# Keeping attention's result in SBUF as fp16 pairs instead of storing it to DRAM and loading it back, in a fused attention and MLP kernel

## Chip, core, metric

One core of a Trainium2 chip. The engines are TensorE (PE), VectorE (DVE), ScalarE (ACT), GpSimd (POOL) and SyncE (SP), which issues nearly all DMAs. The metric is the device time of one execution, in microseconds; lower is better.

## What is computed

```python
# attention, per batch b (4) and head h (8): S=576 tokens, D=64
scores = (q @ k.T) / sqrt(D) + (cum[:, None] - cum[None, :])   # cum = cumsum(log f)
attn = softmax(where(causal, -1e9, scores)) @ v
x = attn as [2304 tokens, 512]
# first MLP: 512 -> 2048 -> 512
g = leaky_relu(x @ moe_w_in, 0.01) ;  y = g @ moe_w_out
# second MLP: 512 -> 1024 -> 512
h = y @ moe2_w_in ;  solu = h * softmax(h)
out = (layernorm(solu) * g_ln) @ moe2_w_out
```

All inputs and the output are float32. The kernel keeps float32-like accuracy with pairs: a value is held as a high half and the rest as a low half, and a product is three matmuls (high by high, high by low, low by high).

## The kernel before

The program does not issue its instructions in the order of its text. Each step is recorded as an operation with an engine (or several to choose from), a duration guess, a priority (a lower number goes first) and the buffers it reads and writes. `Plan.run` (a list scheduler) then walks through modelled time, gives each free engine the ready operation with the best priority whose buffers can be had, and emits it. The order on each engine's queue is fixed by that; on the chip every queue runs strictly in order. `PASSES`, `UN`, `ORDER`, `WIP`, `WOP`, `LD...`, `PP...`, `WEIGHT`, `LAT` and the like are priorities and guesses for this planner. Buffers are tags with a number of slots; when a tag is used up, its slots go over to other tags (`heirs`).

**Attention** runs in eight passes, `PASSES`. Pass A of a batch does query blocks 0 and 1 (tokens 0 to 255) of its four head pairs, pass B blocks 2, 3 and the 64-row block 4. Per head: scores on PE into `ps_s`; mask and row extreme on DVE (L750); exp with row sum on ACT (L700); the guard, which adds 1e-9 to the sum and scales it (L709, L710 on DVE, or L712 ACT, L714 DVE or POOL); reciprocal (L718); high part `hl` (L453, L458) and low part (L464); a DMA transpose `pt<-hl` issued by SP; PV on PE into `ps_v`; eviction into `xr`, float32, on ACT and DVE (L781, L784). `V` is split into pairs in `split_v` (low parts L464 on DVE, or L467 and L468 on POOL).

**The way of x.** `pair` ends with a store of `xr` to the DRAM tensor `xs_d`. The first MLP works on nine token blocks of 256: block b and 4+b are tokens 0 to 255 and 256 to 511 of batch b, block 8 the last 64 tokens of all four batches. `load_x` waits for the stores of all four head pairs of a batch, loads the block back into an `xw` buffer (once `sd`, so the trace says `sd<-xs_d`), and splits it into two fp16 pair tiles `x` (copy L453 or L460, then subtraction L468).

**The first MLP** runs in units `(block, g)`, g being one of two halves of the hidden layer: g=0 holds the first `GA` groups of 256 hidden columns, g=1 the rest of eight. `hidden` makes one group (24 matmuls of 256 columns from `x`, then two ACT and one DVE operation into a pair `g`); after the groups of a unit come its y matmuls, added up in `yo`. Weights come as 32 chunks of 512 KB through three staging buffers `wst`, are joined and reduced on ACT, POOL and DVE, and are split into pairs in `wz` or `qa`. A half's output weights (`split_wo`) are scaled together, so its y matmuls need all chunks of that half. Units of this MLP run on PE between attention's matmuls, as filling, and after attention without a break. **The second MLP** follows, per 128 tokens.

**Start.** `decay` computes the cumulated log of f and writes two rows of 8 KB into `qa`, rows 64 and 65, by two small DMAs (`qa<-sd`); the first scores need them.

Of the kernel before, what the change touches and what calls it, by code (L numbers as in the profile page):

```python
# [7 lines left out]
F32 = mybir.dt.float32  # L8
# [19 lines left out]
NVT = 9  # L28
NRAW = 3
NWST = 3  # L30
ORDER = (0, 1, 4, 2, 5, 3, 6, 8, 7)
EARLY = 1779.78
NE = 2
NQK = 3
WST = 1.0
PA = 83.64

PASSES = (("A", 0, 127.52, 0.5), ("A", 1, 186, 3), ("B", 0, 200, 5), ("A", 2, 222, 8), ("B", 1, 256, 20), ("A", 3, 338, 8), ("B", 2, 372, 20), ("B", 3, 454, 20))
PP = -9.25
PV = -9.04  # L40
SM = 6.0
AV = -2.77
EP = 1726.79
LD = 60.42
LDV = 18.49
LDW = 5.82
KSTEP = 0.56
EPD = 11.22
URGENT = -1000.0
BACKLOG = 9115.27  # L50
LOP = 310.01
WIP = (120.0, 190.0)
WOP = (121.0, 190.14)
WIST = -3.25
WOST = 1.0
WSP = (122.0, 189.01)
GA = 3
UN = ((0, 0), (0, 1), (1, 0), (1, 1))
NYO = 2
NX = 3  # L60
NGT = 4
US0 = 17.36
HST = 2.0
TB = 256
NB = NT // TB
# [5 lines left out]
LNS = 1024.0  # L71
TOP = 14
GS = 2.0 ** -24
YD = 14.21
OLAG = 32.29

# [24 lines left out]
    __slots__ = ("eng", "dur", "emit", "bufs", "prio", "npred", "succ", "seq", "taken", "dma", "weight", "heat", "lock")  # L101


WEIGHT = {"DVE": 4.54}
WEIGHT2 = {"DVE": 1.9}
HEAT = 0.25
TOPE = 253.69
QUEUES = ("SP",)
SHARE = 0.62
PORT = 150.0  # L110
LAT = {"PE": 220.0, "ACT": 150.0, "DVE": 150.0, "POOL": 57}
WINDOW = 4096 / 1.2
HI_ENGS = ("ACT", "DVE")
UNITS = {2: ((0, 1),), 3: ((3,), (2,))}
V_ENGS = ("ACT", "DVE", "POOL")
VL_ENGS = ("DVE", "POOL")
HD4 = 0
REC_ENGS = ("DVE", "POOL", "ACT")
LO_ENGS = ("DVE", "POOL")
# [232 lines left out]
def dve(n):  # L352
    return 1.042 * n + 70
# [26 lines left out]
def body(tc, kqa, kq, vt, f, wa, w2i, w2o, gln, out):  # L380
# [10 lines left out]
    def tiles(pool, name, n, shape, dt):  # L391
        return [pool.tile(shape, dt, name=f"{name}{i}") for i in range(n)]
# [16 lines left out]
    ex = base.tile([128, 128], F32, name="ex")  # L409
    P.tag("ex", [ex])  # L410
    P.tag("turn", [ex])
    junk = base.tile([128, 512], BF16, name="junk")
    P.tag("va", tiles(base, "va", 2, [128, 1], F32R))

    xs_d = tiles(dram, "xs_d", B, [128, KD, S], F32)
    yp_d = tiles(dram, "yp_d", NB, [128, KD, TB], F32)
    dr_d = dram.tile([2 * NP, 4, KQ], F32, name="dr_d")

# [23 lines left out]

    halves = lambda t, dt: [t[:, 512 * j:512 * j + 512].bitcast(dt) for j in range(2)]
    as_g = lambda t: t.bitcast(F16).rearrange("p (j n) -> p j n", j=2)
    heirs("sd", "xw", "xw")
    heirs("dec", *[lambda t: [("g", as_g(t[:, 512 * j:512 * j + 512])) for j in range(2)]] * 2)
    heirs("wst", lambda t: [("yo", t[:, 512 * j:512 * j + 512].bitcast(F32)) for j in range(2)],
          *[lambda t: [(nm, as_g(t[:, 512 * j:512 * j + 512])) for j, nm in enumerate(("g", "x"))]] * 2)
    heirs("qa", lambda t: [("wz", t[:, h, p]) for h in range(2) for p in range(KD)])

    def copy_on(eng, o, i, scale=None):
# [79 lines left out]
    def decay():  # L531
# [161 lines left out]
    def softmax(parts, prio):  # L693
# [127 lines left out]
    def pair(p, prio, blocks):  # L821
        n0 = len(P.ops)
        b, kd = divmod(p, KD)
        full = len(blocks) == 2
        (prep_full if full else prep_split)(p, prio)
        xr = P.buf("xr")
        k = 0
        for hd in range(2):
            pts = {}
            for unit in UNITS[len(blocks)]:  # L830
                pts.update(scores(p, unit, hd, prio + SM + KSTEP * k, full))
                k += 1
# [134 lines left out]
    def load_x(blk, prio):
        xb = []
        deps = [o for b, a, c, o in spills if any(b == x and a <= s < c for x, s, _ in tokens(blk))]
        for q in range(2):  # L970
            xw, x = P.buf("xw"), P.buf("x")
            at = 0
            wide = lambda xw=xw: xw.t[:, 0:512].rearrange("p (a n) -> p a n", a=2)
            for b, s, n in tokens(blk):
                load((xw, at), lambda wide=wide, o=at, n=n: wide()[:, :, o:o + n],
                     lambda q=q, b=b, s=s, n=n: xs_d[b][:, 2 * q:2 * q + 2, s:s + n], 128 * 2 * n * 4, prio - 4000, deps=deps)
                at += n
            src = lambda xw=xw: xw.t[:, 0:512]
            copy_f(lambda x=x: x.t[:, 0], src, 512, prio - 3000, w=[(x, 0)], r=[xw])
            sub_f(lambda x=x: x.t[:, 1], src, lambda x=x: x.t[:, 0], 512, prio - 3000, w=[(x, 1)], r=[xw, (x, 0)])  # L980
            xb.append(x)
        return xb

    YPD, YP = {}, []

    XB, YO, LEFT = {}, {}, {}

    def ffn(blk, g, prio):
        eprio = prio - EP
        first, last = blk not in XB, LEFT.setdefault(blk, 2) == 1  # L990
        LEFT[blk] -= 1
        if blk < B:
            P.op(DVE, 140, lambda: nc.vector.tensor_scalar(ev(YS + 4 * g + blk), ev(EB + blk), ev(EZ + g), WSC * 2.0 ** (40 - 3 * TOP), op0=ALU.mult, op1=ALU.mult),
                 prio - 3000, w=[(EX, ("y", g, blk))], r=[(EX, ("b", blk)), (EX, ("z", g))])
        if first:
            XB[blk], YO[blk], YPD[blk] = load_x(blk, prio), [P.buf("yo") for q in range(2)], []
# [217 lines left out]
```

## Time and profile before

| | us |
|---|---|
| runs of the kernel before: median (lowest to highest of 3) | 789.78 (787.78 to 791.29) |
| the profiled execution: its time | 793.71 |
| the profiled execution: its span, first to last event | 791.9 |
| PE busy with matmuls in that span | 719.5 |
| DVE, ACT, POOL busy | 513.5, 467.3, 285.4 |

Read it so: the span is the time from the first to the last recorded event of one execution; its time includes 1.8 us around it. An engine's idle time is span less busy time. A matmul's end is modelled, so busy stretches of PE say that it was fed, not that it ran at its peak.

### The profile page before, as it was taken

What the parts mean: (1) busy time and instruction counts of PE and PEld (TensorE: products, weight loads), DVE (VectorE), ACT (ScalarE), POOL (GpSimd) and SP (SyncE); (2) the same over time, 40 slices, a digit from 0 to 9 for tenths busy, and PEclk for the clock granted to TensorE, in tenths of its full rate; (3) what the DMA queues carried; (4) which work ended last, traced back from release to release, by engine and by line L of the source; (5) the groups of instructions that cost most, each with busy time, mean ns of one, the idle gap of its engine ahead of it and who ended that gap; (6) DMA issues with size and microseconds to landing.
All of it is one profiled execution on the core that took longest, in us unless ns stands there. A gap on an engine that the chain in (4) does not pass through costs nothing.

```text
span 791.9 us, 15449 instructions
## 1 busy us (share of the span) xinstructions
PE 719.5 (91%) x5647; PEld 576.6 (73%) x5647; DVE 513.5 (65%) x1256; ACT 467.3 (59%) x1060; POOL 285.4 (36%) x341
## 2 busy tenths in 40 slices
PE   2453898999799999999999999999999999999997
PEld 1342787787688877888888888888887766666653
DVE  6888988977888777887883552115134675556651
ACT  2879989876889679988882563224221333233321
POOL 3839696723553076653513220001001233222020
PEclk9999999999999999999999999999999999999999
DMA  8798779568778778777866550000003334453224
GB/s 267 203 240 274 203 189 242 108 117 162 167 172 144 137 153 174 153 132 162 168 129 150 176 201 27 9 20 2 27 1 94 94 94 106 107 107 90 59 65 106
DMA packets 175277, 103.61 MB, mean 131 GB/s; under 512 B 147313, under 2 KB 155713, under 8 KB 175201
## 3 DMA queue, kind: packets, MB, share of 16 engines
q1 hardware_dynamic: 175200, 102.62, 55.8%
q8 instruction: 44, 0.72, 0.4%
q14 instruction: 33, 0.26, 0.1%
HBM read 52.67 MB, written 14.78 MB: 85 GB/s over the span
## 4 chain that ended last, share of the span: by engine, by line
PE 47%; DMA 2%; DVE 1%; ACT 0%; issue 0%; SPq 0%; ACTq 0%
PE ps_f L499 31%; PE ph L499 12%; PE ps_g L499 3%; DMA tr<-hl 1%; DMA pt<-hl 1%; PE ps_v L499 0%; PE ps_s L499 0%; DVE hl L464 0%; ACT ot L1098 0%; SPq L490 0%; DVE st L709 0%; ACT hl L453 0%; DVE ps_s L750 0%; DVE xr L784 0%; DVE st L718 0%
## 5 line engine op out<-in xcount | busy, mean ns | idle before, releaser
L499 PEld LDWEIGHTS <-wz 128*128 128x128 f16 x2808 | 273.6, 99 | 39.5 <-issue 6.8
L499 PE MATMUL ps_f<-x,wz 128*128 128x256 f16 x864 | 108.9, 278 | 0.0
L499 PE MATMUL ph<-w,y 128*128 128x512 f32 x432 | 103.7, 396 | 0.0
L464 DVE SCALAR_TENSOR_TENSOR hl<-ps_s,st,hl 128x512 f16<-128x512 f32 (+4 forms) x160 | 83.4, 538 | 17.3 <-ACT hl L453 15.9
L499 PEld LDWEIGHTS ph<-w,y 128*128 128x128 f32 x432 | 81.0, 188 | 18.1
L499 PE MATMUL ps_f<-wst,wz 128*128 128x256 f16 x696 | 90.0, 273 | 0.0
L700 ACT ACTIVATE ps_s<-ps_s,st 128x512 f32<-128x512 f32 (+4 forms) x160 | 78.4, 490 | 19.2 <-DVE st L750 11.4
L499 PE MATMUL ps_v<-pt,VT 128*128 128x128 f16 (+1 forms) x928 | 60.9, 218 | 28.7 <-DVE xr L784 14.5
L468 POOL TENSOR_TENSOR kq<-raw,kq 64x576 fp32r<-64x576 f32 (+1 forms) x60 | 74.4, 1246 | 25.7 <-ACT kq L453 22.9
L499 PE MATMUL ps_f<-g,wz 128*128 128x256 f16 x636 | 81.3, 273 | 1.3 <-DVE g L953 1.3
L499 PEld LDWEIGHTS <-VT 128*128 128x128 f16 x928 | 53.3, 101 | 38.0 <-issue 20.8
L499 PEld LDWEIGHTS <-tr 128*128 128x128 f16 x432 | 41.0, 98 | 53.0 <-issue 3.9
L453 ACT ACTIVATE hl<-ps_s,st 128x512 f16<-128x512 f32 (+3 forms) x128 | 67.0, 550 | 21.1 <-DMA pt<-hl 10.2
L499 PE MATMUL ps_f<-dec,wz 128*128 128x256 f16 x612 | 77.1, 273 | 0.0
L499 PEld LDWEIGHTS <-qa 128*128 128x128 f16 x648 | 61.9, 98 | 9.6 <-issue 2.5
L750 DVE CUSTOM_DVE_ANT_0 ps_s<-ps_s,mask 128x128 f32<-128x128 f32 (+3 forms) x128 | 62.4, 498 | 9.5 <-PE ps_s L499 7.3
L499 PE MATMUL ps_s<-kq 128*128 128x512 f32 (+5 forms) x256 | 64.3, 376 | 4.4 <-DVE hl L464 2.9
L453 ACT ACTIVATE hl<-raw 128x1024 f16<-128x1024 f32 x17 | 18.0, 1057 | 62.1 <-DMA tr<-hl 32.8
L499 PEld LDWEIGHTS ps_s<-kq 128*128 128x128 f32 (+1 forms) x256 | 41.5, 194 | 12.2 <-DVE hl L464 3.7
L1072 POOL TENSOR_SCALAR s<-s 128x1 f32<-128x1 f32 x18 | 4.4, 245 | 126.2 <-DVE s L1067 125.9
L1055 ACT ACTIVATE raw<-ph,s 128x1024 f32<-128x1024 f32 x18 | 20.0, 1113 | 39.6 <-DVE s L1053 39.6
L952 ACT ACTIVATE ps_f<-ps_f 128x512 f32<-128x512 f32 x72 | 42.5, 590 | 0.4
(176 smaller groups left out, 1193.9 us busy)
## 6 DMA issues: line engine op xcount, KB each, us to landing
wst<-wa SPq DMA_DIRECT2D x32, 512.0 KB
raw<-kq SPq DMA_DIRECT2D x16, 480.0 KB
VT<-vt SPq DMA_DIRECT2D x16, 320.0 KB
raw<-yp_d SPq DMA_DIRECT2D x18, 256.0 KB
sd<-xs_d SPq DMA_DIRECT2D x16, 256.0 KB
raw<-w2i SPq DMA_DIRECT2D x8, 512.0 KB
raw<-w2o SPq DMA_DIRECT2D x8, 512.0 KB
out<-ot SPq DMA_DIRECT2D x16, 256.0 KB
```

The lines of the kernel that those rows point to most:

```text
L453: nc.scalar.activation(o, i, CP, scale=1.0 if scale is None else scale)
L464: nc.vector.scalar_tensor_tensor(o, a, scale, b, op0=ALU.mult, op1=ALU.subtract)
L468: (nc.vector if eng == DVE else nc.gpsimd).tensor_tensor(o, a, b, op=ALU.subtract)
L499: nc.tensor.matmul(o, lhsT=l, rhs=r, start=start, stop=stop)
L700: P.op(ACT, act(W, 1, True) + 93, lambda view=view, j=j, k=k: nc.scalar.activation(view(), view(), AF.Exp, bias=sts.t[:, j:j + 1], scale=- ...
L750: P.op(DVE, dve(W) + 130, lambda i=i, j=j, view=view: nc.vector.tensor_tensor_reduce(view(), view(), mask[:, 512 - 128 * i:640], -0.125, 3 ...
L952: P.op(ACT, act(512, 0, True), lambda: nc.scalar.activation(ps.t, ps.t, AF.Prelu, scale=GS, alpha=0.01), eprio, rw=[ps])
L1055: P.op(ACT, act(1024, 2, True), lambda: nc.scalar.activation(E(), ps.t, AF.Exp, bias=st.t[:, 0:1], accum_out=st.t[:, 1:2]), eprio, w=[Eb, ...
L1072: nc.gpsimd.tensor_scalar(st.t[:, 5:6], st.t[:, 5:6], 1.0e-6, 1.0, op0=ALU.add, op1=ALU.mult)
```

## The change

- **x stays on chip.** `xs_d`, the stores in `pair` and all of `load_x` are gone. Instead each `pair` copies its `xr` into the high halves of the block's `x` tiles (ACT or POOL) and subtracts for the low halves (DVE or POOL): pieces of 256 columns in pass A, of 256 and 64 in pass B. An `x` slot is held from the first pair that writes it until its block's last `hidden`. The three `sd` slots and both halves of two `wst` slots become `x` slots: 10 in the end, where there were 5; `g` gets 8 slots in place of 10.
- **The guard in other forms.** On DVE one 128x2 operation becomes two of 128x1; for block 4, `scalar_tensor_tensor` becomes `tensor_scalar` with a second scalar from memory.
- **The two decay rows** are issued from ACT's queue.
- **Engines and orders.** V's low parts run on DVE alone; the row sums of output weights on DVE or ACT, before on ACT alone. `GA` goes from 3 to 4, the first five chunks (before: two) are loaded with early priority, and units and blocks go in another order: with `UN`, (0,0), (1,0), (0,1), (4,0), (1,1), (4,1) first, and block 8 last instead of 7.
- Many priorities and planner guesses have other values; `VB_ENGS`, `IB_ENGS` and `PVF` leave things as they were.

```diff
-ORDER = (0, 1, 4, 2, 5, 3, 6, 8, 7)
+ORDER = (0, 1, 4, 5, 2, 3, 6, 7, 8)
-NE = 2
+NE = 5
-GA = 3
-UN = ((0, 0), (0, 1), (1, 0), (1, 1))
+GA = 4
+UN = ((0, 0), (1, 0), (0, 1), (4, 0), (1, 1), (4, 1))
+OB_ENGS = ("DVE", "ACT")
+XP = -2.2
+XH_ENGS = ("ACT", "POOL")
+XL_ENGS = ("DVE", "POOL")
+ROWQ = ("ACT",)
-WEIGHT = {"DVE": 4.54}
-WEIGHT2 = {"DVE": 1.9}
+WEIGHT = {"DVE": 7.0}
+WEIGHT2 = {"DVE": 1.75}
-V_ENGS = ("ACT", "DVE", "POOL")
-VL_ENGS = ("DVE", "POOL")
+V_ENGS = ("ACT", "POOL")
+VL_ENGS = ("DVE",)
...
-    heirs("sd", "xw", "xw")
+    heirs("sd", *[lambda t: [("x", as_g(t[:, 0:512]))]] * 3)
...
-          *[lambda t: [(nm, as_g(t[:, 512 * j:512 * j + 512])) for j, nm in enumerate(("g", "x"))]] * 2)
+          *[lambda t: [("x", as_g(t[:, 512 * j:512 * j + 512])) for j in range(2)]] * 2)
...
-                 w=[(bq, k)], r=[(cn, k)])
+                 w=[(bq, k)], r=[(cn, k)], engs=ROWQ)
...
+    def bound(z, n, j, key, prio, engs=(DVE, ACT), **kw):
+
+        def go(e):
+            if e == DVE:
+                top_of(ev(j), z())
+            else:
+                nc.scalar.activation(junk[:, 0:n], z(), AF.Abs, accum_out=ev(j))
+
+        d = {DVE: dve(n), ACT: act(n, 1) + 93}
+        flex(engs, [d[e] for e in engs], go, prio, w=[(EX, key)], **kw)
...
-                nc.vector.scalar_tensor_tensor(scale(), total(), 1.0e-9, sts.t[:, 4:5], op0=ALU.add, op1=ALU.add)
+                nc.vector.tensor_scalar(scale(), total(), 1.0e-9, sts.t[:, 4:5], op0=ALU.add, op1=ALU.add)
...
+            elif e == DVE:
+                for i in range(ns):
+                    nc.vector.tensor_scalar(sts.t[:, 6 + i:7 + i], sts.t[:, 3 + i:4 + i], 1.0e-9, PS, op0=ALU.add, op1=ALU.mult)
...
-        c0, c1 = 128 * blocks[0], min(S, 128 * blocks[-1] + 128)
-        o = move(lambda: xs_d[b][:, kd, c0:c1], lambda: xr.t[:, c0:c1], 128 * (c1 - c0) * 4, prio - 400, r=[xr])
-        spills.append((b, c0, c1, o))
+        for blk, c0, n, t0 in ((b, 0, TB, 0),) if full else ((B + b, TB, TB, 0), (2 * B, 2 * TB, 64, 64 * b)):
+            if len(XB.setdefault(blk, [])) == kd // 2:
+                XB[blk].append(P.buf("x"))
+            x, o = XB[blk][kd // 2], TB * (kd % 2) + t0
+            at = lambda j, x=x, o=o, n=n: x.t[:, j, o:o + n]
+            src = lambda c0=c0, n=n: xr.t[:, c0:c0 + n]
+            copy_f(lambda at=at: at(0), src, n, prio + XP, engs=XH_ENGS, w=[(x, (0, kd, t0))], r=[xr])
+            sub_f(lambda at=at: at(1), src, lambda at=at: at(0), n, prio + XP, engs=XL_ENGS, w=[(x, (1, kd, t0))], r=[xr, (x, (0, kd, t0))])
```

## Rows read from the trace of the kernel before

**Rows 1.** By stretch: length, busy us of PE, PEld, DVE, ACT, POOL, clock, DMA, GB/s.
```profile
0.00:63.00 63.00, 28.85 (x110) 20.88 (x110) 51.83 (x167) 41.51 (x110) 34.89 (x46) 1.00 0.89 243
63.00:80.00 17.00, 4.68 (x23) 3.22 (x24) 14.27 (x32) 16.43 (x34) 15.29 (x14) 1.00 0.87 259
80.00:100.00 20.00, 18.05 (x145) 14.90 (x144) 19.37 (x53) 17.95 (x47) 13.22 (x12) 1.00 0.79 203
100.00:200.00 100.00, 93.84 (x882) 79.83 (x880) 81.52 (x238) 83.12 (x208) 59.22 (x60) 0.98 0.76 165
200.00:300.00 100.00, 90.87 (x863) 78.77 (x861) 80.22 (x234) 81.60 (x209) 46.19 (x49) 0.98 0.78 150
300.00:423.00 123.00, 119.56 (x1200) 103.48 (x1198) 97.18 (x281) 104.21 (x254) 54.43 (x59) 1.00 0.75 149
423.00:770.00 347.00, 347.00 (x2362) 268.36 (x2361) 164.46 (x252) 118.81 (x198) 61.01 (x100) 1.00 0.30 80
770.00:791.90 21.90, 16.66 (x77) 7.19 (x75) 4.66 (x6) 3.69 (x5) 1.20 (x4) 1.00 0.42 96
```

**Rows 2.** Timeline of PE, 80 to 90 us: start, us, instruction, count, [idle before].
```profile
80.11 5.33 PE L499 MATMUL ps_f<-x,wz 128*128 128x256 f16 x24
...
86.84 2.79 PE L499 MATMUL ps_f<-x,wz 128*128 128x256 f16 x24
```

**Rows 3.** Timelines of DVE, SP and POOL: batch 0's last xr, its way through DRAM.
```profile
63.44 0.43 DVE L784 SCALAR_TENSOR_TENSOR xr<-ps_v,xr 64x256 f32<-64x256 f32 x1 [0.30 <-ACT xr L781]
63.90 0.34 SPq L490 DMA_DIRECT2D xs_d<-xr  x1
67.43 0.96 SPq L490 DMA_DIRECT2D sd<-xs_d  x2
73.80 2.77 POOL L468 TENSOR_TENSOR x<-sd,x 128x512 f16<-128x512 f32 x2 [0.17 <-ACT x L453]
```

**Rows 4.** Timelines of SP and POOL: the 16th chunk's load; last split of half 0.
```profile
67.05 0.33 SPq L490 DMA_DIRECT2D wst<-wa  x1
70.22 1.15 POOL L468 TENSOR_TENSOR wz<-wz,wz 128x512 f16<-128x512 f32 x1
```

**Rows 5.** Timelines of SP and PE, 7 to 20 us: decay rows and first scores.
```profile
7.33 2.85 SPq L490 DMA_DIRECT2D qa<-sd  x2
15.97 4.18 PE L499 MATMUL ps_s<-qa 66*128 66x128 f32 x12 [2.83 <-DMA qa<-sd]
```

**Rows 6.** Groups by form, the guards: count | busy us, mean ns | idle before, releaser.
```profile
L714 DVE TENSOR_SCALAR st<-st 128x2 f32<-128x2 f32 x12 | 9.5, 788 | 4.5 <-ACT ps_s L700 4.5
L709 DVE SCALAR_TENSOR_TENSOR st<-st 128x1 f32<-128x1 f32 x16 | 6.4, 402 | 3.9 <-ACT ps_s L700 3.8
L714 DVE TENSOR_SCALAR st<-st 128x1 f32<-128x1 f32 x17 | 2.5, 147 | 1.6 <-ACT ps_s L700 1.5
```

**Rows 7.** The tile VT: instruction x count: ns min/median/max, first and last start, forms.
```profile
L468 POOL TENSOR_TENSOR VT<-VT,VT x14: 1393/1397/1998, 25.6 to 294.9; 128x640 f16<-128x640 f32 x14
L464 DVE SCALAR_TENSOR_TENSOR VT<-VT,ex,VT x2: 854/1313/1772, 35.5 to 83.4; 128x640 f16<-128x640 f32 x2
```

**Rows 8.** The same view of the tile sd: splitting a loaded x.
```profile
L468 POOL TENSOR_TENSOR x<-sd,x x12: 1148/1156/1749, 73.8 to 497.7; 128x512 f16<-128x512 f32 x12
L453 ACT ACTIVATE x<-sd x10: 614/622/632, 73.1 to 497.0; 128x512 f16<-128x512 f32 x10
```

**Rows 9.** The same view of xs_d; then SP's timeline after attention's last store.
```profile
L490 SPq DMA_DIRECT2D xs_d<-xr x32: 319/355/1346, 43.1 to 423.9; - x32
L490 SPq DMA_DIRECT2D sd<-xs_d x24: 371/448/1130, 67.4 to 458.0; - x24
...
424.24 2.03 SPq L490 DMA_DIRECT2D sd<-xs_d  x4
```

**Rows 10.** Who waited for whom on PE: total us, times, longest.
```profile
PE ps_v L499 <- DVE xr L784: 14.5, 9, 5.3
PE ps_v L499 <- DMA pt<-hl: 11.8, 9, 4.4
```

More of the change, by code (lines that the diff above doesn't have):

```diff
@@ L30 @@
 NWST = 3
-ORDER = (0, 1, 4, 2, 5, 3, 6, 8, 7)
+ORDER = (0, 1, 4, 5, 2, 3, 6, 7, 8)
 EARLY = 1779.78
-NE = 2
+NE = 5
 NQK = 3
 WST = 1.0
-PA = 83.64
-PASSES = (("A", 0, 127.52, 0.5), ("A", 1, 186, 3), ("B", 0, 200, 5), ("A", 2, 222, 8), ("B", 1, 256, 20), ("A", 3, 338, 8), ("B", 2, 372, 20), ("B", 3, 454, 20))
-PP = -9.25
+PA = 110.6
+PASSES = (("A", 0, 127.52, 0.5), ("A", 1, 186, 3), ("B", 0, 200, 5), ("A", 2, 222, 8), ("B", 1, 256, 20), ("A", 3, 338, 8), ("B", 2, 373.26, 20), ("B", 3, 454, 15.2))
+PP = 23.22
 PV = -9.04
@@ L43 @@
 EP = 1726.79
-LD = 60.42
+LD = 11.72
 LDV = 18.49
-LDW = 5.82
+LDW = -3.55
 KSTEP = 0.56
@@ L49 @@
 URGENT = -1000.0
-BACKLOG = 9115.27
+BACKLOG = 10469.5
 LOP = 310.01
-WIP = (120.0, 190.0)
-WOP = (121.0, 190.14)
-WIST = -3.25
+WIP = (116.65, 190.0)
+WOP = (121.0, 191.56)
+WIST = 1.0
 WOST = 1.0
-WSP = (122.0, 189.01)
-GA = 3
-UN = ((0, 0), (0, 1), (1, 0), (1, 1))
+WSP = (122.0, 192.0)
+GA = 4
+UN = ((0, 0), (1, 0), (0, 1), (4, 0), (1, 1), (4, 1))
 NYO = 2
+VB_ENGS = ("DVE",)
+IB_ENGS = ("DVE",)
+OB_ENGS = ("DVE", "ACT")
[3 more added lines that the diff above has]
+ROWQ = ("ACT",)
+PVF = 0
 NX = 3
 NGT = 4
-US0 = 17.36
+US0 = 20.0
 HST = 2.0
@@ L73 @@
 GS = 2.0 ** -24
-YD = 14.21
-OLAG = 32.29
+YD = 9.0
+OLAG = 33.39
 WSC = 256.0
@@ L101 @@
     __slots__ = ("eng", "dur", "emit", "bufs", "prio", "npred", "succ", "seq", "taken", "dma", "weight", "heat", "lock")
-WEIGHT = {"DVE": 4.54}
-WEIGHT2 = {"DVE": 1.9}
+WEIGHT = {"DVE": 7.0}
+WEIGHT2 = {"DVE": 1.75}
 HEAT = 0.25
-TOPE = 253.69
+TOPE = 267.42
 QUEUES = ("SP",)
@@ L110 @@
 PORT = 150.0
-LAT = {"PE": 220.0, "ACT": 150.0, "DVE": 150.0, "POOL": 57}
+LAT = {"PE": 220.0, "ACT": 150.0, "DVE": 150.0, "POOL": 80.0}
 WINDOW = 4096 / 1.2
@@ L411, in body @@
     P.tag("turn", [ex])
-    junk = base.tile([128, 512], BF16, name="junk")
+    junk = base.tile([128, 640], BF16, name="junk")
     P.tag("va", tiles(base, "va", 2, [128, 1], F32R))
-    xs_d = tiles(dram, "xs_d", B, [128, KD, S], F32)
     yp_d = tiles(dram, "yp_d", NB, [128, KD, TB], F32)
@@ L585, in body @@
     st, QK, VT, QA = {}, {}, {}, {}
-    attn_ops, spills = [], []
+    attn_ops, XB = [], {}
     def load_qa():
@@ L665, in prep_v @@
         move(lambda: vr.t, lambda: vt[p], 128 * 640 * 4, prio - LDV, w=[vr, (TURN[b], i)])
-        P.op(DVE, dve(640), lambda: top_of(ev(EV + 5 * b + i), vr.t), prio + PV, r=[vr], w=[(EX, ("v", p))])
+        bound(lambda: vr.t, 640, EV + 5 * b + i, ("v", p), prio + PV, VB_ENGS, r=[vr])
     def split_v(b, prio):
@@ L712, in guard @@
                 nc.scalar.activation(scale(), total(), CP, scale=PS, bias=1.0e-9 * PS)
+            elif e == DVE:
+                for i in range(ns):
+                    nc.vector.tensor_scalar(sts.t[:, 6 + i:7 + i], sts.t[:, 3 + i:4 + i], 1.0e-9, PS, op0=ALU.add, op1=ALU.mult)
             else:
-                (nc.vector if e == DVE else nc.gpsimd).tensor_scalar(scale(), total(), 1.0e-9, PS, op0=ALU.add, op1=ALU.mult)
+                nc.gpsimd.tensor_scalar(scale(), total(), 1.0e-9, PS, op0=ALU.add, op1=ALU.mult)
         engs = (DVE,) if one and nb == 2 else REC_ENGS
@@ L792, in pv @@
     def pv(p, hd, pts, xr, prio):
-        ps, blocks = P.buf("ps_v"), sorted(pts)
+        ps, blocks = P.buf("ps_f" if p < PVF else "ps_v"), sorted(pts)
         bufs = {id(b): b for b, _ in pts.values()}
@@ L875, in sums @@
     def sums(z, j, prio):
-        P.op(ACT, act(512, 1), lambda: nc.scalar.activation(junk, z.t, AF.Abs, accum_out=ev(j)), prio, w=[(EX, ("m", j))], r=[z])
+        P.op(ACT, act(512, 1), lambda: nc.scalar.activation(junk[:, 0:512], z.t, AF.Abs, accum_out=ev(j)), prio, w=[(EX, ("m", j))], r=[z])
     WI, WO, W2I, W2O, ZO, ZQ = {}, {}, {}, {}, {}, {}
@@ L888, in load_wi @@
             zs.append(z)
-            P.op(DVE, dve(512), lambda z=z, i=i: top_of(ev(EM + 3 * k + i), z.t), prio, w=[(EX, ("i", c))], r=[z])
+            bound(lambda z=z: z.t, 512, EM + 3 * k + i, ("i", c), prio, IB_ENGS, r=[z])
         power(EM + 3 * k, 3, [(EX, ("i", 2 * k + i)) for i in range(2)], EK + k, ("k", k), prio)
@@ L897, in load_wo @@
         ZO[c] = whole(wa[c, 1], prio)
-        sums(ZO[c], EO + c + (c >= 2 * GA), prio)
+        j = EO + c + (c >= 2 * GA)
+        bound(lambda: ZO[c].t, 512, j, ("m", j), prio, OB_ENGS, r=[ZO[c]])
     GRP = (range(GA), range(GA, NG))
@@ L965, in tokens @@
         return [(blk % B, TB * (blk // B), TB)] if blk < 2 * B else [(b, S - 64, 64) for b in range(B)]
[L967 to L982, printed above, removed]
     YPD, YP = {}, []
-    XB, YO, LEFT = {}, {}, {}
+    YO, LEFT = {}, {}
     def ffn(blk, g, prio):
         eprio = prio - EP
-        first, last = blk not in XB, LEFT.setdefault(blk, 2) == 1
+        first, last = blk not in YO, LEFT.setdefault(blk, 2) == 1
         LEFT[blk] -= 1
@@ L995, in ffn @@
         if first:
-            XB[blk], YO[blk], YPD[blk] = load_x(blk, prio), [P.buf("yo") for q in range(2)], []
+            YO[blk], YPD[blk] = [P.buf("yo") for q in range(2)], []
         gs = {k: hidden(k, XB[blk], prio + HST * i, eprio + i) for i, k in enumerate(GRP[g])}
```

## Prediction, made before the changed kernel was run

> **What bounds the kernel now.** I read the busy time by stretch first, then PE's timeline up to 110 us, then the other engines' timelines for what PE waited for, and last the groups by form for prices. The reader is to see in [rows 1] that PE is busy for all 347.0 of the 347 us from 423 to 770: there the kernel is fed matmuls without a gap and nothing but fewer or faster matmuls helps. The change removes no matmul. So the whole room is PE's idle time elsewhere, window less busy time in [rows 1]: 34.2 us before 63, 12.3 from 63 to 80, 2.0 from 80 to 100, 6.2 from 100 to 200, 9.1 from 200 to 300, 3.4 from 300 to 423 and 5.2 behind 770, in all 72.4. A microsecond of idle that gets filled with first-MLP matmuls is a microsecond off the end, since the same matmuls are then missing from the dense part. A delay of attention, on the other hand, costs nothing as long as PE has MLP work to do instead.
>
> The largest single piece with one cause is 63 to 80. The first matmul of the first MLP starts at 80.11 [rows 2]; from there to 770 PE stays at 90% and more [rows 1]. What it waited for is in [rows 3]: the last `xr` of batch 0 is evicted at 63.44 + 0.43 = 63.87, stored at 63.90, the two loads are issued at 67.43, and POOL ends the second subtraction at 73.80 + 2.77 = 76.57. From `xr` to `x` is 12.7 us, and PE's queue takes 3.5 more to come to it.
>
> **The change part by part.** All sums are against the profiled execution, 793.71 us (span 791.9). It lies 3.9 above the median of the runs, 789.78, which I take as the base: a saving is taken off that.
>
> *No round trip.* The high copy of the last 256-column piece costs ACT less than the 0.62 of 512 columns, and the subtraction POOL less than 1.16 [rows 8]; halves are 0.31 and 0.58. ACT is busy 16.4 and POOL 15.3 of the 17 us [rows 1], so I add 2 us of queueing: `x` is there at 63.87 + 0.3 + 0.6 + 2.0 = 66.8. The bounds are 65 (no queueing) and 75 (as late as now but for the DMA). PE can start at 66.8 instead of 80.1: 13.3 us, of which attention's matmuls take at most the 4.7 of that stretch [rows 1], leaving 8.6. Is there work for it? With `GA` 4 the first unit has four hidden groups of 24 matmuls, 2.79 us each when PE runs at full rate, but the first took 5.33 [rows 2]. The granted clock of that stretch reads 1.00, the 2.4 GHz level [rows 1], so the column does not show why; I take the durations. The slow first group is paid at 80 now and at 67 then, so it cancels. Four groups, 11 us, fill the hole: **-8.5**, bounds -12.3 (all of it) and -3.
>
> *GA 4.* The unit's y matmuls now need 16 chunks instead of 12. The 16th is issued at 67.05 now, and the last split of the 12 ends at 70.22 + 1.15 = 71.4 [rows 4]. Four more splits of output weights cost POOL something like 1.15 each and as much again before it, so y is ready near 80, when the hidden groups end (66.8 + 11 + 2.5 + attention's 4). Nearly hidden; if the cover is gone, PE idles again. **+1**, bounds 0 and +6.
>
> *Decay rows on ACT's queue, more early chunks.* The two issues hold SP from 7.33 to 10.18, and the first scores start at 15.97 after a wait of 2.83 for these rows [rows 5]. They can come at most that much earlier; three early chunks (1.5 MB, 5.8 us at the 259 GB/s of [rows 1]) can push the loads of k and V later. ACT waits instead of SP; behind it stand exps that need these scores anyway, and weight steps. Bounds -2.8 and +5.8; between them I take **-0.5**. A rule of the Trainium skill speaks against even this: in "DMA: Bandwidth & Descriptors", section "Issuing engines are not separate DMA queues", all issuers share the same 16 DMA engines, and another issuer saves only the time of issuing. By it the rows would land no more than the second issue's share of those 2.85 us earlier, and the sum would move by under 1 us. No run shown here has such a DMA on ACT's queue.
>
> *Guards.* Twelve 128x2 operations at 788 ns become 24 at the 147 ns of the 128x1 form: -5.9 us of DVE; sixteen at 402 fall to about 147: -4.1 [rows 6]. DVE is busy 344 of the first 423 us (81%) [rows 1], PE mostly not waiting for it: **-0.5**, bounds -3 and 0.
>
> *V's low parts on DVE.* Fourteen move from POOL at 1.40 to DVE at 0.85 to 1.77 [rows 7]: DVE +12 to +25. *Splitting x inside attention.* Now the last loads are issued from 424.24 to 458.0 [rows 9], ten of 24 by that timeline, so about four of the eighteen splits lie behind attention; now all lie before it, in 48 narrow pieces instead of 18 wide ones. Four times (0.62 + 1.16) [rows 8] is 7 us, and up to as much again for the pieces, on ACT and POOL. Cover: MLP matmuls on PE. Together **+1.5**, bounds 0 and +19 (rival 3).
>
> *Fewer DMAs.* SP loses 32 stores at 0.36 and 24 loads at 0.45 us [rows 9], 22 us of issue time in front of its transposes. PE waited 11.8 us for `pt<-hl` and 14.5 for `xr` [rows 10]. **-1.5**, bounds -5 and 0.
>
> *Slots.* Ten `x` slots hold five blocks, and block 8 holds two from batch 0's pass B to the end. A shortage delays attention, and PE does MLP work meanwhile: 0, at worst +4. *The end.* Block 8 last makes the last stores two of 128 KB instead of one of 256: 0, within 1.
>
> Sum: -8.5 + 1 - 0.5 - 0.5 + 1.5 - 1.5 = -8.5. 789.8 - 8.5 = **781.3**.
>
> **The rivals.** *1. The start moves as a whole.* The rows' wait goes (-2.8), the hole closes entirely (-12.3), transposes and guards give -4: 770.7. For it: PE is idle for over half of the first 63 us, and SP's queue is in order. Against: DVE is busy 51.8 of these 63 us [rows 1], and the weights' conversions it does are all still there.
>
> *2. The hole is filled and opens again.* `x` comes early, but output weights of half 0 (16 chunks) or block 1's `x` do not; PE runs out after four hidden groups and idles before 100 for about what it saved: 789.8 - 1.5 = 788.3. For it: ACT, POOL and DVE are over 83% busy from 63 to 80 [rows 1], and MLP evictions now come on top. Against: 16 chunks are issued by 67.05 even now [rows 4].
>
> *3. DVE becomes the bound in attention (slower).* V's low parts at the long price, 14 x 1.77 = 24.8, and up to 16 row sums at the 0.85 of the nearest DVE row, 13.7, less the guards' 10.0: 344 + 28.5 = 373 of 423 us, 88%. PE's queue is in order: MLP work standing behind a score or PV matmul that waits for DVE waits too. If idle from 100 to 423 doubles (+18.7), the time is 789.8 - 8.5 + 18.7 = 800. It decides once more than 12.5 us of idle are added there. For it: `xr` on DVE is what PE waits for longest in [rows 10]. Against: PE idles only 3.4 of the 123 us from 300 [rows 1], with DVE at 79%. A rule of the Trainium skill goes with this rival ("SBUF — State Buffer", section "Who interferes with whom"): a DVE operation with two SBUF inputs and a GpSimd one that reads SBUF exclude each other, the later one waiting for all of the first. The two DVE rows of the low part, 854 and 1772 ns for the same form [rows 7], agree with it; by the rule most of the fourteen would cost the long price, as this rival has it.
>
> **How the numbers follow.** A measurement of this kernel can tell about 0.5%, 3.9 us, from no change: faster is below 785.8, slower above 793.7. Forecast: 0.55, with its own range 774 to 786. Rival 1: 0.13, 767 to 774. Rival 2: 0.19, 786 to 792, a tenth of it below 785.8. Rival 3: 0.13, above 793.7. Faster 0.55 + 0.13 + 0.02 = 0.70, same 0.17, slower 0.13. The range 767 to 791 leaves out rival 3, the end of rival 2 and a little at the bottom.
>
> **What would show it.** Right: in the changed profile the first matmuls on `x` start between 65 and 70 us instead of 80.11; PE idle from 63 to 80 falls from 12.3 to about 4; idle from 100 to 423 stays near 18.7; PE is dense to the tail and the span is near 783. The round-trip step is wrong if the first of them start after 75, the `GA` step if a new gap of over 4 us stands between 80 and 105 with a weight or `x` as releaser, the DVE step if idle from 100 to 423 grows beyond 30 us. The first 63 us tell rival 1: idle well below 30.

## The result, and the profile after

The changed kernel takes 770.53 us (median of 4 runs, 767.32 to 771.52); the kernel before, timed beside it, 790.53 (4 runs). The ratio is 0.973, with a 95% interval from 0.9666 to 0.9793: faster by 20.0 us. The prediction was 781.3, so the sign and the range (767 to 791) held, and the size was 10.8 us too small: the measured time lies below the forecast's own range (774 to 786), in that of rival 1. The profiled execution after took 767.32 (span 765.5). It lies 3.2 below its median, and before's profiled one lay 3.2 above the median that was timed beside it; of the 26.4 us between the two spans, 20 are therefore between the medians.

The kernel after, by stretch, with the columns of [rows 1]; what was the dense stretch to 770 now ends at 744:

```profile
0.00:63.00 63.00, 25.69 (x96) 18.00 (x96) 51.64 (x149) 38.17 (x102) 32.91 (x49) 1.00 0.90 250
63.00:80.00 17.00, 11.26 (x72) 8.88 (x73) 15.41 (x51) 15.90 (x44) 14.05 (x16) 1.00 0.66 185
80.00:100.00 20.00, 16.18 (x147) 13.96 (x146) 18.00 (x54) 19.26 (x52) 15.29 (x15) 1.00 0.66 165
100.00:200.00 100.00, 97.04 (x943) 85.48 (x943) 81.30 (x233) 84.06 (x212) 70.85 (x81) 1.00 0.67 155
200.00:300.00 100.00, 98.84 (x950) 86.28 (x948) 79.77 (x247) 84.58 (x231) 48.34 (x70) 1.00 0.64 134
300.00:423.00 123.00, 123.00 (x1257) 109.30 (x1256) 90.41 (x265) 99.63 (x252) 61.75 (x80) 1.00 0.64 129
423.00:744.00 321.00, 321.00 (x2122) 244.79 (x2120) 155.79 (x238) 111.66 (x184) 53.08 (x95) 1.00 0.29 78
744.00:765.50 21.50, 16.07 (x74) 6.95 (x72) 4.06 (x6) 3.69 (x5) 1.20 (x4) 0.98 0.42 98
```

Window less PE's busy time gives PE's idle time. Against [rows 1] it went from 34.2 to 37.3 before 63 us, from 12.3 to 5.7 up to 80, from 2.0 to 3.8 up to 100, then from 6.2 to 3.0, from 9.1 to 1.2 and from 3.4 to 0.0 up to 423, and from 5.2 to 5.4 in the tail: 72.4 to 56.4, 16.0 less. So the start of the kernel got a little worse. The hole that the prediction was about gave 6.6, and attention's main part, from 100 to 423, where it expected nothing, gave 14.6. The other 10.4 us are busy time: 719.5 before, 709.1 after, for 5647 matmuls recorded in both. The clock column stood at 0.98 from 100 to 300 in [rows 1] and reads 1.00 here, up to 744: an estimated 3.7 of the 10.4 (2% of the 184.7 us that PE was busy there). Where the other 6.7 lie was not found.

The timeline of PE after:

```profile
16.37 0.47 PE L506 MATMUL ps_f<-ident,va 128*128 128x128 f32 x1 [16.37 <-DVE va L648]
17.13 2.47 PE L506 MATMUL ps_s<-qa 66*128 66x128 f32 x8 [0.29 <-DMA qa<-sd]
...
71.46 4.68 PE L506 MATMUL ps_f<-x,wz 128*128 128x256 f16 x24
...
90.78 2.46 PE L506 MATMUL ps_f<-g,wz 128*128 128x256 f16 x21
...
112.15 3.45 PE L506 MATMUL ps_f<-x,wz 128*128 128x256 f16 x30
115.44 0.82 PE L506 MATMUL ps_f<-sd,wz 128*128 128x256 f16 x6
```

The first MLP starts at 71.46 instead of 80.11 [rows 2], and y of the first unit at 90.78. Of the 30 matmuls from 112.15, 24 are one more group of block 0, whose two tiles are both called `x`; unit (1,0), block 1's first half, begins with the last six, at about 114.8 (an `x` in a former `sd` slot is called `sd` here). POOL's timeline shows when the last piece of each `x` was there, the first line for block 0, the second for block 1:

```profile
69.53 1.24 POOL L475 TENSOR_TENSOR x<-xr,x 128x256 f16<-128x256 f32 x1
...
111.95 1.12 POOL L475 TENSOR_TENSOR sd<-xr,sd 128x256 f16<-128x256 f32 x1
```

Block 0's last split ends at 70.77 (76.57 by [rows 3]), block 1's at 113.07. PE's waits after, with the columns of [rows 10]:

```profile
PE ps_v L506 <- DMA pt<-hl: 5.9, 3, 2.1
...
PE ps_v L506 <- DVE xr L805: 3.4, 3, 2.0
```

Both waits of [rows 10] shrank, 11.8 to 5.9 and 14.5 to 3.4 us.

### The profile page after: what moved, and what is told of

Same layout as the page of the kernel before. It is cut to its first block, busy times and chain, and to the rows that moved or that the text cites. A ratio compares the mean times of both kernels' runs of the same rounds, so it can differ in the third digit from the quotient of the medians.

```text
span 765.5 us, 15379 instructions
## 1 busy us (share of the span) xinstructions
PE 709.1 (93%) x5647; PEld 573.7 (75%) x5647; DVE 496.4 (65%) x1236; ACT 456.9 (60%) x1075; POOL 297.5 (39%) x406
## 4 chain that ended last, share of the span: by engine, by line
PE 65%; ACT 3%; DVE 2%; issue 1%; DMA 1%; POOL 0%; ACTq 0%; DVEq 0%
PE ps_f L506 42%; PE ph L506 13%; PE ps_s L506 4%; PE ps_v L506 3%; PE ps_g L506 3%; ACT ps_s L718 1%; ACT hl L460 1%; DMA pt<-hl 1%; DVE hl L471 0%; ACT kq L460 0%; DVE ps_s L771 0%; DVE VT L471 0%; ACT ot L1108 0%; ACT xr L802 0%; DVE xr L805 0%
## 5 line engine op out<-in xcount | busy, mean ns | idle before, releaser
L506 PEld LDWEIGHTS <-wz 128*128 128x128 f16 x2700 | 261.1, 98 | 37.2 <-issue 6.7
L506 PE MATMUL ps_f<-dec,wz 128*128 128x256 f16 x768 | 99.0, 273 | 0.9 <-DVE g L980 0.9
L506 PE MATMUL ps_f<-g,wz 128*128 128x256 f16 x636 | 85.9, 273 | 0.0
L506 PEld LDWEIGHTS <-qa 128*128 128x128 f16 x756 | 73.3, 98 | 9.5 <-issue 1.1
L460 ACT ACTIVATE hl<-ps_s,st 128x512 f16<-128x512 f32 (+4 forms) x148 | 73.4, 531 | 11.2 <-DVE st L739 5.2
L506 PE MATMUL ps_f<-x,wz 128*128 128x256 f16 x576 | 70.9, 277 | 0.0
L506 PE MATMUL ps_s<-kq 128*128 128x512 f32 (+5 forms) x256 | 60.9, 366 | 2.4 <-DVE hl L471 1.9
L980 DVE TENSOR_TENSOR g<-ps_f,g 128x512 f16<-128x512 f32 x35 | 24.1, 689 | 39.1 <-ACT ps_f L979 39.0
L506 PE MATMUL ps_f<-sd,wz 128*128 128x256 f16 x360 | 49.1, 273 | 0.0
L506 PE MATMUL ps_f<-wst,wz 128*128 128x256 f16 x360 | 46.2, 273 | 0.0
```

The costliest lines, as they stand in the source:

```text
L460: nc.scalar.activation(o, i, CP, scale=1.0 if scale is None else scale)
L506: nc.tensor.matmul(o, lhsT=l, rhs=r, start=start, stop=stop)
L980: P.op(DVE, dve(512) + 60, lambda: nc.vector.tensor_tensor(g.t[:, 1], ps.t, g.t[:, 0], op=ALU.subtract), eprio, w=[(g, 1)], r=[ps, (g, 0)])
```

## The experiments

Every edit to this kernel makes the planner lay out all queues anew, unless the operations and their guesses stay the same. The first experiment prices that; the next two change the guard inside an unchanged order.

**Another order, the same work.**

```diff
-PORT = 150.0
+PORT = 140.0
```

> The changed kernel with one guess of the planner moved a little (PORT 150 to 140), which puts nearly all queues in another order and changes no work. Theory D (any order that this planner was not trimmed for loses, whatever the edit): 8 to 25 us slower than the changed kernel. Theory B (x on chip itself holds the gain): within 6 us of it.

777.99 us, ratio 0.9829 (0.9793 to 0.9864). A planner guess moved by 7% and nothing else costs 7.5 us. So a variant of this kernel whose queues come out in another order can be told from the changed one only if it differs by well over that. By stretch:

```profile
80.00:100.00 20.00, 13.30 (x104) 10.73 (x102) 17.58 (x59) 19.66 (x44) 17.42 (x18) 0.81 0.61 158
100.00:200.00 100.00, 96.38 (x898) 83.28 (x897) 80.42 (x235) 88.95 (x224) 72.78 (x86) 0.95 0.69 153
```

PE got 43 matmuls fewer done from 80 to 100 and 45 fewer in the next 100 us, at a lower clock in both.

**The guard alone, in the kernel before.** The queues keep before's order.

```diff
-                nc.vector.scalar_tensor_tensor(scale(), total(), 1.0e-9, sts.t[:, 4:5], op0=ALU.add, op1=ALU.add)
+                nc.vector.tensor_scalar(scale(), total(), 1.0e-9, sts.t[:, 4:5], op0=ALU.add, op1=ALU.add)
...
+            elif e == DVE:
+                for i in range(ns):
+                    nc.vector.tensor_scalar(sts.t[:, 6 + i:7 + i], sts.t[:, 3 + i:4 + i], 1.0e-9, PS, op0=ALU.add, op1=ALU.mult)
```

> The kernel before with only the guard's new forms on DVE; every queue keeps its order, instruction for instruction, but for the guards. Theory A (the guard is a large part: a 128x2 guard can stand behind several GpSimd operations, 2.80 us at 200.0 in the trace of before, and the 5.3 us hole of PE and the lower clock that follow are its doing): 4 to 9 us faster than before, no DVE guard over 0.3 us, PE idle from 200 to 225 at most 2 us instead of 5.3. Theory B (the forecast: guards are worth 0.5 us; x on chip is what pays): within 2 us of before.

788.85 us over 12 runs beside 791.59 over 23: ratio 0.9962 (0.9934 to 0.999), 3 us. The interval leaves out 1. More than the 0.5 that the prediction gave it. A stretch of the kernel before that the prediction didn't read shows a place where such a gain can come from, timelines of POOL, DVE and PE:

```profile
199.11 1.41 POOL L468 TENSOR_TENSOR kq<-raw,kq 64x576 fp32r<-64x576 f32 x1
200.48 1.15 POOL L468 TENSOR_TENSOR x<-sd,x 128x512 f16<-128x512 f32 x1
201.60 1.15 POOL L468 TENSOR_TENSOR wst<-sd,wst 128x512 f16<-128x512 f32 x1
...
200.00 2.80 DVE L714 TENSOR_SCALAR st<-st 128x2 f32<-128x2 f32 x1
...
208.18 0.75 PE L499 MATMUL ps_v<-pt,VT 128*128 128x128 f16 x6 [5.30 <-DVE xr L784]
```

An operation on 256 numbers stands on DVE for 2.80 us, until POOL's third instruction in a row ends; 5.4 us later PE breaks a 5.30 us wait for an `xr` of DVE. The same place in the guard-only kernel:

```profile
199.28 0.20 DVE L715 TENSOR_SCALAR st<-st 128x1 f32<-128x1 f32 x2
...
204.81 0.50 PE L499 MATMUL ps_v<-pt,VT 128*128 128x128 f16 x6 [3.31 <-DVE xr L787]
```

The guard's two halves take 0.20 us, and PE's wait is 2 us shorter; most of it is still there, so it has another cause besides. PE's idle time from 200 to 225 fell from 5.3 to 4.3 us, where theory A wanted 2 at most. The 3 us lie between the two theories.

**The old guard, in the changed kernel.** The same edit backwards, in after's order.

> The changed kernel with the guard's old forms; the queues keep their order. Theory A: 4 to 9 us slower than the changed kernel (ratio to before 0.978 to 0.985), DVE guards of over 1 us again. Theory B: within 2 us of the changed kernel (ratio to before 0.970 to 0.976).

772.61 us, ratio 0.9755 (0.9719 to 0.9791), beside 0.973 (0.9666 to 0.9793): 2 us, and the intervals overlap, so nothing that can be told here. Its group by form of the wide guards:

```profile
L732 DVE TENSOR_SCALAR st<-st 128x2 f32<-128x2 f32 x7 | 2.5, 355 | 1.0 <-ACT ps_s L718 0.8
```

In this order only seven of the wide guards are on DVE, at 355 ns instead of the 788 of [rows 6]: what the guard costs depends on what POOL does beside it (the last section shows it for the kernel before).

**The decay rows back on SP's queue, in the changed kernel.**

```diff
-ROWQ = ("ACT",)
+ROWQ = ("SP",)
```

> The changed kernel with the two decay rows issued from SP's queue again (the queues are planned anew). If ACT's queue is worth what the wait for the rows was (up to 3 us): first scores 1 to 3 us later and 1 to 6 us slower than the changed kernel. If it is worth nothing: within what a new order does, as n1_replan showed (7 us), and first scores no later.

778.0 us, ratio 0.9854 (0.9791 to 0.9918), 7.5 above the changed kernel: what another order alone costs, so no price for the queue follows. The mechanism can be read, though: PE's timeline and its stretch from 80 to 100 in this kernel, and the issue of the rows in the changed kernel's timeline of ACT:

```profile
16.19 4.18 PE L506 MATMUL ps_s<-qa 66*128 66x128 f32 x12 [2.56 <-DMA qa<-sd]
...
66.06 3.91 PE L506 MATMUL ps_f<-x,wz 128*128 128x256 f16 x24
...
92.21 3.82 PE L506 MATMUL ps_f<-g,wz 128*128 128x256 f16 x18
...
80.00:100.00 20.00, 12.82 (x91) 9.80 (x90) 18.47 (x46) 17.24 (x48) 15.78 (x16) 0.74 0.55 125
...
7.52 4.29 ACTq L497 DMA_DIRECT2D qa<-sd  x2
```

With the rows on SP the first scores come at 16.19, with them on ACT's queue at 17.13: nothing came earlier. The two issues took 4.29 us on ACT's queue, 2.85 on SP's in [rows 5]. The first MLP starts 5.4 us earlier here than in the changed kernel, and the kernel is slower all the same: y of the first unit starts at 92.21, no earlier than there, and before it PE is idle for 7.2 of the 20 us from 80 to 100, at a granted clock of 0.74.

**x on chip, in all of before's numbers.** The changed code (with the new guard), and before's priorities, guesses, engines, unit order, `GA`, `NE` and `ROWQ`; in short:

```diff
-ORDER = (0, 1, 4, 5, 2, 3, 6, 7, 8)
-NE = 5
-GA = 4
-UN = ((0, 0), (1, 0), (0, 1), (4, 0), (1, 1), (4, 1))
+ORDER = (0, 1, 4, 2, 5, 3, 6, 8, 7)
+NE = 2
+GA = 3
+UN = ((0, 0), (0, 1), (1, 0), (1, 1))
...
-VL_ENGS = ("DVE",)
+VL_ENGS = ("DVE", "POOL")
```

> x kept on chip and the new guard, but every planner number, engine choice, unit order, GA, NE and the queue of the decay rows as before. Theory B: 8 to 12 us faster than before, the first MLP matmul at 65 to 72 us. Theory C (the gain comes from new orders and numbers; the hole before the first MLP matmul only moves): no faster than the guard alone.

803.95 us, ratio 1.0141 (1.0101 to 1.0182): slower than before, and 15 us slower than the guard-only kernel, from which it differs by the way of x with its slots, one guess of the planner (the row sums of output weights, 93 ns longer) and the order that follows. By stretch, then PE's waits from 100 to 200, PE's timeline and SP's:

```profile
100.00:200.00 100.00, 80.71 (x656) 66.34 (x654) 71.12 (x200) 75.84 (x180) 59.75 (x64) 0.85 0.56 133
...
PE ps_v L506 <- DMA pt<-hl: 8.4, 3, 3.7
...
PE ps_f L506 <- POOL wz L475: 1.1, 1, 1.1
...
67.89 1.70 PE L506 MATMUL ps_f<-x,wz 128*128 128x256 f16 x7
...
149.07 0.37 SPq L497 DMA_DIRECT2D wst<-wa  x1
```

The first MLP starts 12 us earlier than in [rows 2], as the round-trip step says. But from 100 to 200 PE does 656 matmuls, where [rows 1] has 882 and the changed kernel 943. Of its 19.3 us of idle time there a weight ends 1.1; the rest are waits for `pt<-hl` (8.4), `va`, `xr` and `yo`. The last weight chunk is issued at 149.07 (before at 131.9, after at 132.1).

**The same, with the changed kernel's unit order.**

```diff
-ORDER = (0, 1, 4, 2, 5, 3, 6, 8, 7)
-NE = 2
-GA = 3
-UN = ((0, 0), (0, 1), (1, 0), (1, 1))
+ORDER = (0, 1, 4, 5, 2, 3, 6, 7, 8)
+NE = 5
+GA = 4
+UN = ((0, 0), (1, 0), (0, 1), (4, 0), (1, 1), (4, 1))
```

> The kernel of run e3_xchip (x on chip and new guard in before's numbers) with the changed kernel's ORDER, UN, GA and NE. Theory E: 10 us or more faster than e3_xchip (804), PE idle from 100 to 200 at most 8 us. Theory D: 785 to 810, no nearer to the changed kernel.

781.9 us, ratio 0.9867 (0.9834 to 0.9901): 22 us faster than without these four lines. The stretch is full again:

```profile
100.00:200.00 100.00, 97.12 (x937) 84.97 (x936) 80.09 (x231) 82.11 (x206) 50.68 (x59) 1.00 0.65 145
```

**That unit order with x through DRAM**, the same four lines on the guard-only kernel.

> The kernel of run e1_guard (x through DRAM, before's numbers, new guard) with the changed kernel's ORDER, UN, GA and NE: the missing corner beside e1_guard, e3_xchip and e8_xchip_units. Theory H (x on chip and the unit order pay only together): no faster than e1_guard (789), and 8 us or more slower than e8_xchip_units (782). Theory I (the unit order pays by itself): 778 to 784.

802.36 us, ratio 1.0155 (1.0078 to 1.0232): without x on chip the same lines cost 14 us. From 115 to 130, with the last split of block 1's `x` and its first matmuls, first in the run before (x on chip):

```profile
115.00:130.00 15.00, 15.00 (x147) 13.53 (x146) 10.60 (x25) 14.76 (x32) 11.02 (x11) 1.00 0.82 231
...
115.13 1.07 POOL L475 TENSOR_TENSOR sd<-xr,sd 128x256 f16<-128x256 f32 x1
...
117.95 0.82 PE L506 MATMUL ps_f<-x,wz 128*128 128x256 f16 x6
```

Then through DRAM, with its timelines of SP, POOL and PE:

```profile
115.00:130.00 15.00, 7.89 (x59) 5.45 (x56) 11.06 (x27) 14.04 (x35) 11.27 (x11) 0.89 0.71 211
...
115.49 0.93 SPq L490 DMA_DIRECT2D sd<-xs_d  x2
...
131.03 1.54 POOL L468 TENSOR_TENSOR x<-sd,x 128x512 f16<-128x512 f32 x1
...
123.53 2.74 PE L499 MATMUL ps_f<-x,wz 128*128 128x256 f16 x12 [1.71 <-POOL wz L468]
...
135.95 4.97 PE L499 MATMUL ps_f<-x,wz 128*128 128x256 f16 x24
```

The second unit is now (1,0), which needs block 1's `x`. On chip its last piece is split at 116.20 and the unit starts at 117.95, with weights that unit (0,0) has used already: 147 matmuls from 115 to 130. Through DRAM `x` is loaded at 115.49 and split only at 132.57, and its matmuls start at 135.95. Until then only block 0 has an `x`, so PE does block 0's second half, whose weights are still being split: it waits 3.8 us for `wz` and does 59 matmuls.

**The two crossed in the changed kernel.** Its x through DRAM again (`load_x`, the stores and before's slots back, all numbers of the changed kernel kept):

> The changed kernel with x through DRAM again (stores, loads and splits as before, with before's slots), all else as changed. Theory B: 8 to 13 us slower than the changed kernel (ratio to before 0.983 to 0.99), the first MLP matmul at 80 or later. Theory C: within 4 us of the changed kernel.

795.44 us, ratio 1.0047 (1.0019 to 1.0075). And its x on chip with before's `ORDER`, `NE`, `GA` and `UN`:

> The changed kernel with ORDER, UN, GA and NE of before; x on chip, guard and all other numbers as changed. Theory E (the unit order is what lets x on chip pay, since it gives PE units to do before half 1's weights are there): 10 to 25 us slower than the changed kernel, with a gap or low clock between 100 and 200 us. Theory B: within 6 us.

792.41 us, ratio 0.9987 (0.9964 to 1.0011). Either takes the whole gain away, 25 and 22 us, three times what another order costs. From 100 to 200, the former's row first:

```profile
100.00:200.00 100.00, 87.33 (x792) 74.39 (x791) 77.83 (x242) 88.19 (x219) 70.19 (x72) 0.93 0.79 178
...
100.00:200.00 100.00, 88.65 (x768) 74.30 (x767) 81.20 (x248) 88.42 (x225) 76.22 (x89) 0.90 0.75 167
```

**Which of the four lines.** `UN` alone, on the kernel with x on chip in before's numbers:

```diff
-UN = ((0, 0), (0, 1), (1, 0), (1, 1))
+UN = ((0, 0), (1, 0), (0, 1), (4, 0), (1, 1), (4, 1))
```

> The kernel of run e3_xchip with the changed UN alone: unit (1,0) is put ahead of (0,1), GA, NE and ORDER stay. Theory E in its narrow form (PE needs a unit that does not wait for half 1's weights): most of the 22 us between e3_xchip and e8_xchip_units, so 780 to 790, and over 850 PE instructions in matmuls from 100 to 200 us instead of 656. If GA or NE does it: within 6 us of 804.

807.13 us, ratio 1.0211 (1.0141 to 1.028). It is not `UN` by itself: 676 matmuls from 100 to 200, against 937 with all four.

```profile
100.00:200.00 100.00, 80.33 (x676) 66.92 (x674) 73.61 (x204) 77.04 (x183) 61.27 (x66) 0.86 0.57 133
```

**Slots.** Two more for `x` and two fewer for `g`, then two more for `g` and two fewer for weights, both on the kernel with x on chip in before's numbers:

```diff
-NX = 3
-NGT = 4
+NX = 5
+NGT = 2
```

> The kernel of run e3_xchip with two more x slots from the start and two fewer g slots. Theory F (x slots: blocks 0, 1, 4 and 8 want eight, and there are six until the weight loads end, so attention waits and PE runs dry between 100 and 200 us): 8 to 15 us faster than e3_xchip. Otherwise within 5 us of it, or as far off as a new order makes it.

815.61 us, ratio 1.0311 (1.0274 to 1.0347), 598 matmuls from 100 to 200. The run trades one kind of slot for another, so it shows only that `x` slots paid for with `g` slots do not help.

```diff
-NWZ = 27
-NGT = 4
+NWZ = 25
+NGT = 6
```

> The kernel of run e3_xchip with two more g slots from the start, paid for with two wz slots. Theory G (unit (0,1) holds five of eight g slots until half 1's output weights are there, and PE finds no hidden group to do; two g slots fewer cost 12 us in run e10_slots): 5 to 15 us faster than e3_xchip. If g slots do not bind: within 6 us of 804, or slower for the missing wz slots.

798.25 us, ratio 1.011 (1.0035 to 1.0185), 732 matmuls. By the two ratios (1.011 and 1.0141) 2 us better than without, no more than another order can do.

## Why the prediction was right in sign and too small

Four of the runs form a square, all in before's other numbers and with the new guard (ratio to the kernel before):

| | before's unit order | the changed unit order |
|---|---|---|
| x through DRAM | 0.9962 | 1.0155 |
| x on chip | 1.0141 | 0.9867 |

Each alone costs 14 to 15 us, both together gain 7.5. Had the two simply added up, the last field would be 1.0141 + 1.0155 - 0.9962 = 1.0334; it is 0.0467, or 37 us, lower. The 7.5 that both gain is itself no more than another order can do, and only the first field keeps the order of the kernel before, so a part of the two losses may be due to a new order as such; the 37 us are five times that.

PE's idle time from 100 to 423, in one execution of each, goes the same way: in the order of the fields 13.8 and 24.2, 24.0 and 10.2 us. In the changed kernel it is 4.1, and 17.5 and 14.4 with x through DRAM and with before's unit order. The changed kernel's other numbers and engines take the last field on to 0.973, another 11 us. These were not divided, since another order alone moves 7.5.

*No round trip, -8.5.* As a step about one hole it was right in kind and too large: the first matmul of the MLP came 8.6 us earlier, not 13.3, at 71.46 where 66.8 was expected, since the last `xr` of batch 0 came 2.1 us later (66.00) and POOL did two copies and a subtraction for K before the last split, which ended at 70.77. In the changed kernel with x through DRAM it came at 81.60. Idle from 63 to 80 fell by 6.6, not 8.5. As a price for the edit it was wrong: with before's unit order the edit costs 15 us, with the new one it gains 20 to 25.

*GA 4, +1.* The gap of over 4 us between 80 and 105 that would have shown it wrong did not come: the longest is 2.02 us, for `xr`. But y started at 90.78, not near 80, and it starts hardly earlier where the hidden groups do: 92.21 with the decay rows on SP (first MLP at 66.06), 89.69 with x on chip and the new unit order in before's numbers (63.25). What holds y there is not shown.

*The step that failed* is that the sum has no term for the order of the units. Only `GA` was priced (+1), by the weights of the first unit, and the forecast said "idle from 100 to 423 stays near 18.7". It fell to 4.1. Unit (1,0) as the second one takes weights that are there already, but needs block 1's `x` at about 115; on chip it is split at 113.07 (116.20 in before's numbers), through DRAM at 132.57. That half of the square is shown by the traces. Why x on chip loses in before's order is not shown: the second unit there is (0,1), but weights end only 1.1 of PE's 19.3 us of waits from 100 to 200. The last chunk comes 17 us later than before, and the last piece of block 1's `x` at 129.27, 13 us later than with the new unit order. What delays these, and which of `GA`, `NE` and `ORDER` is needed beside `UN`, stays open.

*Rival 2* did not happen in the changed kernel, where idle from 80 to 100 rose only from 2.0 to 3.8 us. It can be seen in two other runs: after its four hidden groups PE is idle for 7.2 us from 80 to 100 with the decay rows on SP, and for 6.9 with x on chip and the new unit order in before's numbers, though what ends these waits is `xr`, `va` and `hl` of DVE. Its other half, block 1's `x` that does not come, is the run through DRAM with the new unit order.

*Rival 1* named the time that was measured, 770.7, by a mechanism that did not take place: idle in the first 63 us is 37.3, and was to be well below 30. The range reached down to 767 for this rival's sake, and no term of the sum has the 14.6 us; that the measured time lies inside it is luck.

*Rival 3* fell. V's low parts cost DVE 17.6 us; the tile VT of the changed kernel:

```profile
L471 DVE SCALAR_TENSOR_TENSOR VT<-VT,ex,VT x16: 868/884/1702, 26.6 to 283.6; 128x640 f16<-128x640 f32 x16
```

Most took the short time of [rows 7], where the rival wanted the long one, and DVE's busy time up to 423 fell from 344.4 to 336.5 us. The +1.5 for V's low parts and the splitting of x has no run of its own.

*Guards, -0.5:* 3 us in before's order, and in after's order 2, which can't be told from nothing. The term reckoned with DVE's busy time, not with single long waits of a small operation. *Decay rows, -0.5:* the wait for them on PE fell from 2.83 [rows 5] to 0.29 us, but the first scores came at 17.13 instead of 15.97. The wait got shorter because PE's wait before it, for DVE's `va`, lasts to 16.37 us instead of 12.66. The rule of the Trainium skill that the prediction set against this step ("DMA: Bandwidth & Descriptors", "Issuing engines are not separate DMA queues": another issuer saves only the time of issuing) agrees with that. *Fewer DMAs, -1.5:* the waits for `pt<-hl` and `xr` fell by 17.0 us together, but they fell inside a changed order, and no run takes them apart. *Slots, 0:* more `x` slots did not help where `g` slots paid for them; no run has them alone.

Where the 26.4 us of the two spans lie is thus plain (16.0 idle, 10.4 busy); to whom they belong is settled for the pair of x on chip and unit order, and not beyond it.

## What to carry to other kernels

Price a shorter way for data together with the order in which that data is used: ask what the consumer does next with each order, and when its operand is there. Where a planner lays out the queues, first measure what a new order without any change costs (here 7.5 us), and call nothing an effect that is not well above it. A full engine's stretch loses twice when it runs dry, by the gap and by the lower clock after it, so count matmuls done by stretch rather than idle time alone.

## What the runs showed of the hardware

**The clock after a gap.** The kernel with x on chip in before's numbers, by stretches of 5 us, and two groups of its PE timeline:

```profile
120.00:125.00 5.00, 2.06 (x16) 1.58 (x15) 2.43 (x9) 4.89 (x11) 4.17 (x5) 0.77 0.09 36
...
135.00:140.00 5.00, 5.00 (x20) 4.03 (x20) 3.38 (x12) 4.85 (x12) 1.78 (x3) 0.50 0.77 206
...
145.00:150.00 5.00, 5.00 (x45) 4.30 (x43) 4.90 (x11) 4.68 (x15) 2.88 (x4) 1.00 0.73 174
...
138.27 1.49 PE L506 MATMUL ps_f<-x,wz 128*128 128x256 f16 x6
...
144.75 0.82 PE L506 MATMUL ps_f<-sd,wz 128*128 128x256 f16 x6
```

From 120 to 125 PE was busy for 2.06 of 5 us, and from 130 to 135 for 2.12; from 135 to 140 it was busy throughout, at a granted clock of 0.50, the 1.2 GHz level, and six matmuls took 1.49 us. At 1.00, the 2.4 GHz level, six take 0.82. The same came again at 155: after 1.35 us busy out of 5 the clock was 0.50 from 155 to 160. This is part of where the changed kernel's shorter busy time comes from, the 3.7 us estimated above: at no stretch up to 744 does its row show less than 1.00.

**A small DVE operation behind POOL.** The tile `st`, the guards in the kernel before and then in the changed one (ns: least, median, most):

```profile
L714 DVE TENSOR_SCALAR st<-st x29: 135/154/2801, 29.3 to 391.9; 128x1 f32<-128x1 f32 x17, 128x2 f32<-128x2 f32 x12
L709 DVE SCALAR_TENSOR_TENSOR st<-st x16: 140/160/1037, 120.9 to 409.4; 128x1 f32<-128x1 f32 x16
...
L733 DVE TENSOR_SCALAR st<-st x28: 132/153/156, 63.3 to 404.1; 128x1 f32<-128x1 f32 x28
L727 DVE TENSOR_SCALAR st<-st x16: 201/214/214, 106.5 to 400.1; 128x1 f32<-128x1 f32 x16
```

In the first row the timelines of DVE and POOL tell the forms apart. Of the twelve with two elements per partition, two met no POOL instruction and took 169 ns; the other ten took 238 to 2801, and each ended 20 to 57 ns after a POOL instruction did. Nine of them waited for one POOL instruction; the one of 2801 waited for the rest of one and two more behind it. The 17 with one element took 155 at most, with POOL beside them or not. One element is not enough by itself: block 4's old form, `scalar_tensor_tensor` with two operands of that size, took up to 1037 (second row); its new form, `tensor_scalar` with the second as a scalar, took 201 to 214. The old median was 160, so the new form gains only where the old one had to wait.

The Trainium skill ("SBUF — State Buffer", "Who interferes with whom") says that a `tensor_scalar` in a mode with two ports and a GpSimd instruction exclude each other, the later waiting for the first. Nine of the ten agree; the tenth also waited for two instructions that POOL started after it.
